# Sums over keys formed for four tiles at once in place of two, and some thirty further moves of single jobs in the planned order

## The chip, the cores and the metric

One core of one Trainium2 chip. The metric is the time of one execution on the device in microseconds. Five engines work side by side: TensorE (PE, with its weight loads PEld), VectorE (DVE), ScalarE (ACT), GpSimd (POOL) and SyncE (SP), which issues most of the transfers.

## The reference, cut to what matters

One transformer block in float32 with 2048 tokens of width 512: a linear attention, then a mixture of 8 experts of width 1792 to which every token goes. The change lies in the attention and in the order around it:

```python
h = x + A(layernorm(x))          # attention, 32 heads of 16
h2 = h + B(layernorm(h))         # experts
# A:
q, k, v = split_heads(x @ wqkv)
phi_q = concat(softmax(q @ w_phi), softmax(-(q @ w_phi)))   # per head, 32 features
phi_k = concat(softmax(k @ w_phi), softmax(-(k @ w_phi)))
kv = einsum("bhsf,bhsd->bhfd", phi_k, v)     # a sum over all 2048 keys
z  = einsum("bhsf->bhf", phi_k)              # likewise
o  = (phi_q @ kv) / (phi_q @ z + 1e-6)
return o @ wo
# B: gates = softmax(x @ wg), then for every expert gelu(x @ w1) @ w2, weighted by its gate
```

## The kernel before, in words

The tokens are 16 tiles of 128 rows (`NT`). The program has two stages. Up to about 310 us it computes the attention, the second layernorm, the gates and the first product of the experts, in an order of single jobs; behind that it runs the experts in a fixed loop.

**A matmul in float32 precision** is three passes: `mm3` (lines 66 to 75) takes a high and a low part of both sides and issues low by high (L73), high by low (L74) and high by high (L75). A projection of one tile (`project`, L224) is four such triples, so 12 passes. The key weights and the query weights are first multiplied with w_phi ("fold"), so the projections of keys and queries give the arguments of the softmax at once.

**A key tile** t runs through: x stats, x root, x norm, x trans (four transposes, L221, on TensorE), x high (L257, ScalarE) and x low (VectorE), which give the two parts of x; k proj and v proj (TensorE); v ones (L272, a memset of POOL that takes the buffer of the values and sets its column of ones) and v copy; k range (maxima and minima, L234 and L235, VectorE), k below (L239, VectorE) and k above (L242, POOL); k exp, k sums, k scale (L301, POOL).

**The sums over keys** are `k_add` (L302 to L309): for each of the 32 heads one matmul of 128 by 32 features with 128 by 17 values (16 and the column of ones), 32 instructions of four records each in the trace, so 128 records a tile. They add up in one PSUM bank over all 16 tiles, and nobody reads the bank before the last one. Job `("k add", t)` does this for `KB` = 2 tiles, t - 1 and t, in one block, eight blocks in all (t = 1, 3, ... 15). It also gives back the slots of both tiles' features and values.

**A query tile** runs through q proj (12 passes), q copy (L316, ScalarE), q range (VectorE), q subs (L239 and L242, POOL), q exp (ScalarE), q sums (VectorE), q scale (L340 and L341, POOL), and two q trans of four transposes each (L348, TensorE) with their q turned (ScalarE). Tiles 0 to 7 do so between the key tiles; tiles 8 to 15 come behind them and in a row. Then come, by groups of four tiles, q den (L378: denominators), their way to HBM and back (den out, den in), q num (L403: the key-value products), the output projection (out), the second layernorm (h stats to h trans and h turned), the gates (gate, gate copy, ... gate store at L507, whose rows go to HBM), and the products of the first expert (product). Beside it VectorE and ScalarE prepare the experts' first w1 blocks (L610 to L627) and sums of w2 (L644, whose loads are L587); the 16 loads of the output weights are L128, the second loads of x L426 (load r), the loads of w1 and w2 are SP's.

**What sets the order.** Each of these steps is a job with an engine, an estimated cost, the jobs that it must follow, a due time, and the slots that it takes and gives. `plan()` is a list scheduler in Python that makes one order of all jobs from that, within the slots of the pools (43 of `s4`, 15 of `s2`, four PSUM banks of `ps`, four of `pacc`). On that order a list `MOVES` is then applied, pair by pair: the first job is taken out and put right in front of the second. Then the jobs are issued one after the other, and each instruction of an engine is tied behind the one before it, so each engine runs its jobs in exactly this order. Waits between engines follow from the data and from the reuse of slots. The order of the issue is all that the list can change:

```python
order = [name for _, name in plan()]
for name, before in MOVES:
    order.remove(name)
    order.insert(order.index(before), name)
...
for name in order:
    n = len(traced)
    jobs[name][4]()
```

`jobs[name][4]` is the function that issues the job's instructions. A buffer in the program's names (`s_438`, `ps`, `pacc`) is a slot in SBUF or a bank in PSUM.

Of the kernel before, what the change touches and what calls it, by code (L numbers as in the profile page):

```python
# [21 lines left out]
def block_kernel(ctx: ExitStack, tc: tile.TileContext, x, wqkv, w_phi, wo, wg, w1, w2, out):  # L22
# [6 lines left out]
    NT = S // P  # L29
# [62 lines left out]
    st, low = {}, {}  # L92
# [416 lines left out]
    X = {}  # L509
# [487 lines left out]
    jobs, made = {}, []  # L997
# [11 lines left out]
    KB = 2  # L1009
# [431 lines left out]
    order = [name for _, name in plan()]  # L1441
# [3 lines that stand above are left out]
    at = {name: i for i, name in enumerate(order)}  # L1445
    assert all(at[d] < at[n] for n in jobs for d in jobs[n][3])

    assert max(at[n] for n in jobs if n[0] in ("den", "q proj", ("q trans", 1))) < min(at[("num", i), 3] for i in range(2))
    assert max(at[("num", i), 3] for i in range(2)) < at["product", 0, 0]
    for name in order:  # L1450
        n = len(traced)
        jobs[name][4]()
        if name[0] == "m" or len(traced) == n:
            continue
        for ins in traced[n:]:
            if ins.engine in issued:
                tc.add_manual_dep(ins, issued[ins.engine].name,
                                  mybir.DependencyInfo(mybir.DependencyClass.NoSync, mybir.DependencyReason.DATA),
                                  reason="planned order")
            issued[ins.engine] = ins  # L1460
# [28 lines left out]
```

## Time and profile before

| what | us |
|---|---|
| three runs | 2301.76, 2304.96, 2301.81 (median 2301.81) |
| the profiled execution | 2302.05 |
| its span in the trace | 2300.3 |
| TensorE busy, matmul / weight load | 2290.2 / 1998.8 |
| VectorE busy | 2116.5 |
| ScalarE busy | 1762.1 |
| POOL busy | 535.4 |

The span is the trace of the profiled execution, from its first to its last instruction; the execution's own time is 1.75 us longer. Times in the trace count from the span's start. Where the trace shows several instructions of one kind in a row as one line, `x4` is their number, and the duration runs from the first start to the last end. A matmul's duration overlaps with the next one's; how densely they are issued is read from the distance of their starts.

### The profile page before, as it was taken

To read this page: it belongs to the slowest core of one execution; us is meant where nothing else is said; L and a number is where in the kernel's file an instruction comes from. 1 tells how busy PE (TensorE), PEld (TensorE's weight loads), DVE (VectorE), ACT (ScalarE), POOL (GpSimd) and SP (SyncE) were. 2 spreads that over 40 slices of the span, in tenths; PEclk is the share of its full clock that TensorE was granted. 3 is DMA by queue.
4 is the path that set the end of the run, shared out by engine and by line. 5 is a ranking of instruction groups with operands and counts; after the bars stand their busy time and mean duration, and the time that the engine had idled before them with its cause. 6 is when DMAs were issued, how large, how long until landed. Compare 5 with 4: busy or idle time off the path is not lost.

```text
span 2300.3 us, 34809 instructions
## 1 busy us (share of the span) xinstructions
PE 2290.2 (100%) x12544; PEld 1998.8 (87%) x12544; DVE 2116.5 (92%) x3040; ACT 1762.1 (77%) x2934; POOL 535.4 (23%) x688
## 2 busy tenths in 40 slices
PE   9999999999999999999999999999999999999999
PEld 8888888888888888888888888888888888888887
DVE  8878999999999999999998999899999999999998
ACT  6646788877778777777877888877777777777874
POOL 6766211111111111111111421211111111111121
PEclk9999999999999999999999999999999999999999
DMA  3018468888888888888888998998888888878888
GB/s 125 25 49 273 151 164 165 157 165 158 175 165 161 166 157 168 165 161 174 148 177 197 214 193 170 215 197 174 151 178 159 156 175 149 176 153 177 165 162 186
DMA packets 182044, 379.36 MB, mean 165 GB/s; under 512 B 15568, under 2 KB 88912, under 8 KB 181840
## 3 DMA queue, kind: packets, MB, share of 16 engines
q0 software_dynamic: 63776, 210.79, 55.5%
q1 hardware_dynamic: 116768, 166.16, 22.3%
q8 instruction: 99, 1.62, 0.3%
q14 instruction: 73, 0.60, 0.1%
q10 hardware_dynamic: 1328, 0.18, 0.0%
HBM read 161.53 MB, written 224.99 MB: 168 GB/s over the span
## 4 chain that ended last, share of the span: by engine, by line
PE 80%; issue 3%; DMA 3%; DVE 1%; POOL 1%; ACT 0%; POOLq 0%; DVEq 0%; SPq 0%; ACTq 0%
PE ps L73 13%; PE ps L74 13%; PE ps L75 13%; PE pacc L75 13%; PE pacc L73 13%; PE pacc L74 13%; DMA acc1m<-acc1m 1%; DMA acc1m<-s 1%; DVE s L63 1%; DMA h<-s 1%; POOL acc1m L696 1%; PE pacc L793 0%; DMA s<-acc1m 0%; ACT s L694 0%; DVE s L655 0%
## 5 line engine op out<-in xcount | busy, mean ns | idle before, releaser
L63 DVE TENSOR_TENSOR s<-s,s 128x1024 fp32r<-128x1024 f32 (+1 forms) x789 | 743.0, 955 | 87.9 <-ACT s L62 79.0
L62 ACT ACTIVATE s<-s 128x1024 fp32r<-128x1024 f32 (+1 forms) x789 | 660.0, 842 | 12.2 <-DVE s L655 6.4
L73 PE MATMUL pacc<-s,s 128*128 128x512 f32 x1728 | 657.2, 380 | 0.7 <-DVE s L63 0.7
L74 PE MATMUL pacc<-s,s 128*128 128x512 f32 x1728 | 655.1, 379 | 0.4 <-DVE s L63 0.4
L75 PE MATMUL pacc<-s,s 128*128 128x512 f32 x1728 | 654.9, 379 | 0.0
L73 PE MATMUL ps<-s,s 128*128 128x512 f32 x1664 | 633.9, 381 | 1.4 <-DVE s L706 0.5
L74 PE MATMUL ps<-s,s 128*128 128x512 f32 x1664 | 631.0, 379 | 0.6 <-DVE s L63 0.6
L75 PE MATMUL ps<-s,s 128*128 128x512 f32 x1664 | 630.5, 379 | 0.0
L694 ACT ACTIVATE s<-pacc 128x512 f32<-128x512 f32 x756 | 441.5, 593 | 142.1 <-PE pacc L75 137.8
L705 ACT ACTIVATE ps<-ps 128x512 f32<-128x512 f32 x440 | 252.9, 585 | 172.5 <-DVE ps L748 116.2
L73 PEld LDWEIGHTS pacc<-s,s 128*128 128x128 f32 x1728 | 326.5, 189 | 47.9 <-issue 2.2
L74 PEld LDWEIGHTS pacc<-s,s 128*128 128x128 f32 x1728 | 326.6, 189 | 46.7 <-DVE s L63 1.0
L75 PEld LDWEIGHTS pacc<-s,s 128*128 128x128 f32 x1728 | 326.6, 189 | 46.3
L73 PEld LDWEIGHTS ps<-s,s 128*128 128x128 f32 x1664 | 314.4, 189 | 50.1 <-issue 1.5
L74 PEld LDWEIGHTS ps<-s,s 128*128 128x128 f32 x1664 | 314.6, 189 | 44.7 <-DVE s L63 1.3
L75 PEld LDWEIGHTS ps<-s,s 128*128 128x128 f32 x1664 | 314.5, 189 | 44.5
L696 POOL DMA_DIRECT2D acc0m<-s x189 | 162.2, 858 | 812.8 <-ACT s L694 792.3
L706 DVE TENSOR_TENSOR s<-ps,s 128x512 f32<-128x512 f32 x440 | 297.9, 686 | 37.9 <-ACT ps L705 32.6
L696 POOL DMA_DIRECT2D acc1m<-s x175 | 149.4, 855 | 727.4 <-ACT s L694 707.3
L655 DVE TENSOR_TENSOR s<-s,s 128x1024 f32<-128x1024 f32 x224 | 272.8, 1218 | 0.1
L710 ACT ACTIVATE ps<-ps 128x512 f32<-128x512 f32 x226 | 133.2, 589 | 52.2 <-PE ps L75 49.8
L627 DVE TENSOR_TENSOR s<-s,s 128x1024 fp32r<-128x1024 f32 x111 | 136.2, 1227 | 1.5 <-ACT s L625 1.5
(146 smaller groups left out, 1746.7 us busy)
## 6 DMA issues: line engine op xcount, KB each, us to landing
acc0m<-s POOLq DMA_DIRECT2D x196, 512.0 KB, 5.6
acc1m<-s POOLq DMA_DIRECT2D x184, 512.0 KB, 5.7
s<-in_B_w_dram SPq DMA_DIRECT2D x224, 256.0 KB
s<-in_B_w_dram SPq DMA_DIRECT2D x111, 512.0 KB
s<-cwT SPq DMA_DIRECT2D x16, 512.0 KB
s<-in_A_x_dram SPq DMA_DIRECT2D x16, 256.0 KB
s<-in_A_x_dram SPq DMA_DIRECT2D x8, 512.0 KB
rden<-sq SPq DMA_DIRECT2D x16, 256.0 KB
```

Of the source, the lines that this page charges most:

```text
L62: nc.scalar.activation(hi, src, AF.Copy)
L63: return eng.tensor_tensor(lo, src, hi.bitcast(F32), op=ALU.subtract)
L73: nc.tensor.matmul(out_, al, bh, start=first, stop=False, skip_group_check=True)
L74: nc.tensor.matmul(out_, ah, bl, start=False, stop=False, skip_group_check=True)
L75: nc.tensor.matmul(out_, ah, bh, start=False, stop=last, skip_group_check=True)
L627: nc.vector.tensor_tensor(sl, s, sh.bitcast(F32), op=ALU.subtract)
L655: nc.vector.tensor_tensor(r, B[a], B[b], op=ALU.subtract)
L694: nc.scalar.activation(e[:, d], p[d], AF.Copy)
L696: return nc.gpsimd.dma_start(macc[h, m], e, accum_op=ALU.add)
L705: nc.scalar.activation(src, src, AF.Gelu_apprx_tanh)
L706: nc.vector.tensor_tensor(B[b][:, q % 2], src, CW[h, e][:, int(b[2]) - 1], op=ALU.mult)
L710: nc.scalar.activation(dst, src, AF.Copy)
```

## The change

Behind `MOVES` a loop pairs the blocks of the sums: the blocks of k add 1, 5, 9 and 13 are taken from the order, and their instructions are issued at the place of k add 3, 7, 11 and 15, in front of that block's own. So there are four blocks of four tiles. The planner itself doesn't know of it: it plans with `KB` = 2 as before, and the list of slots given back is as it was. The list has 334 pairs in place of 302: eight are gone, 40 are added at its end. In the diff each pair of the list has a line of its own here, and "..." stands for pairs that are not told of.

```diff
     MOVES = [
...
-        (('gate store', 0), ('gate store', 1)),
-        (('h turned', 10), ('X high', 't4')),
-        (('h store', 6), ('keep', 'b11')),
-        ((('q turned', 1), 10), (('q turned', 1), 11)),
-        ('key values', ('q copy', 13)),
...
+        (('product', 0, 0), ('h trans', 10)),
+        (('q exp', 14), (('q turned', 0), 10)),
+        (('load r', 1), ('den out', 0)),
+        ((('q trans', 0), 9), (('q trans', 0), 8)),
+        (('h trans', 11), ('gate back', 1)),
+        (('h turned', 14), ('h turned', 13)),
+        (('fold', 'q', 3), ('v proj', 0)),
+        (('h store', 5), ('gate store', 1)),
+        (('q proj', 9), ('v proj', 14)),
+        ((('q trans', 1), 11), (('q trans', 1), 8)),
+        (('h turned', 8), ('h turned', 11)),
+        (('k add', 15), ('q proj', 10)),
+        ((('q trans', 0), 10), ('q proj', 15)),
...
     ]
...
+    for t in range(KB - 1, NT, 2 * KB):
+        first, then = jobs["k add", t][4], jobs["k add", t + KB]
+        order.remove(("k add", t))
+        then[4] = lambda f=first, g=then[4]: (f(), g())
     for name in order:
```

On TensorE, between a query projection (into `ps`) and the next key projection (into `pacc`), the two blocks of the first four tiles become one (the block of 39.6 us stood earlier, between the query projection and the key projection before these). In a row of L308, the first name is a tile's features and the second its values; `x32` are the 32 heads:

```order
 L74 MATMUL ps<-s_438,s_467 128x512
 L75 MATMUL ps<-s_438,s_467 128x512
-L308 MATMUL pacc<-s_410,s_562 32x17 x32
-L308 MATMUL pacc<-s_485,s_708 32x17 x32
+L308 MATMUL pacc<-s_245,s_344 32x17 x32
+L308 MATMUL pacc<-s_319,s_413 32x17 x32
+L308 MATMUL pacc<-s_415,s_562 32x17 x32
+L308 MATMUL pacc<-s_485,s_644 32x17 x32
 L73 MATMUL pacc<-s_243,s_581 128x512
 L74 MATMUL pacc<-s_243,s_581 128x512
```

The block that stood here for two tiles now holds four; the values lie in other slots, since the first two tiles keep theirs longer.

The last block on TensorE, before: between the query projection of tile 10 (x in `s_1284`) and that of tile 11 (`s_1463`), the sums of tiles 14 and 15:

```order
L73 MATMUL ps<-s_438,s_1284 128x512
L74 MATMUL ps<-s_438,s_1284 128x512
L75 MATMUL ps<-s_438,s_1284 128x512
L308 MATMUL pacc<-s_1737,s_1941 32x17 x32
L308 MATMUL pacc<-s_1864,s_2033 32x17 x32
L73 MATMUL ps<-s_422,s_1463 128x512
L74 MATMUL ps<-s_422,s_1463 128x512
L75 MATMUL ps<-s_422,s_1463 128x512
```

And with the change, behind the query projection of tile 8 (`s_1014`) and in front of that of tile 10 (`s_1220`):

```order
L74 MATMUL ps<-s_438,s_1014 128x512
L75 MATMUL ps<-s_438,s_1014 128x512
L308 MATMUL pacc<-s_1572,s_1703 32x17 x32
L308 MATMUL pacc<-s_1609,s_1888 32x17 x32
L308 MATMUL pacc<-s_1673,s_1941 32x17 x32
L308 MATMUL pacc<-s_1864,s_1982 32x17 x32
L73 MATMUL ps<-s_422,s_1220 128x512
L74 MATMUL ps<-s_422,s_1220 128x512
```

It now has tiles 12 to 15, and query projection 9, which stood in front of 10, is already done before value projection 14.

TensorE's last query transposes, before, from the last denominators of the second group (L378) to the first key-value products (L403); `s_2284` are the features of tile 11, `s_2123` of tile 8, `s_2219` of 10, `s_2310` of 12, `s_2368` of 13, and `x4` is one half of a tile:

```order
L378 MATMUL ps<-s_1774,s_116 32x128
L348 MATMUL ps<-ident,s_2284 128x128 x4
L348 MATMUL ps<-ident,s_2123 128x128 x4
L348 MATMUL ps<-ident,s_2219 128x128 x4
L348 MATMUL ps<-ident,s_2284 128x128 x4
L348 MATMUL ps<-ident,s_2310 128x128 x8
L348 MATMUL ps<-ident,s_2368 128x128 x8
L403 MATMUL ps<-s_963,s_115 32x128 x8
```

And with the change, where `s_2187` is tile 8, `s_2206` tile 10 and `s_2314` tile 12:

```order
L378 MATMUL ps<-s_1710,s_116 32x128
L348 MATMUL ps<-ident,s_2187 128x128 x4
L348 MATMUL ps<-ident,s_2284 128x128 x4
L348 MATMUL ps<-ident,s_2206 128x128 x4
L348 MATMUL ps<-ident,s_2284 128x128 x4
L348 MATMUL ps<-ident,s_2314 128x128 x8
L348 MATMUL ps<-ident,s_2368 128x128 x8
L403 MATMUL ps<-s_963,s_115 32x128 x8
```

The four halves of tiles 8, 10 and 11 stand in another order; the number of transposes is the same, and tiles 12 and 13 stay last. On VectorE and POOL no job changes its place. On ScalarE query exponential 14 is two places further up, q turned 0 of tile 11 stands in front of q turned 1 of tile 10, h turned 11 and 8 change places, and so do h turned 14 and 13. On SP load r 1 stands before den out 0, the first gate's store before the load of w2, and h store 5 before the second gate's store.

## Rows read from the trace of the kernel before

**Rows 1.** The page: busy time of each engine in us, its share of the span and its number of instructions; and the chain of work that ended last, by engine.

```profile
PE 2290.2 (100%) x12544; PEld 1998.8 (87%) x12544; DVE 2116.5 (92%) x3040; ACT 1762.1 (77%) x2934; POOL 535.4 (23%) x688
...
PE 80%; issue 3%; DMA 3%; DVE 1%; POOL 1%; ACT 0%; POOLq 0%; DVEq 0%; SPq 0%; ACTq 0%
```

**Rows 2.** Busy time by stretch, 310 to 2300 us: length, then busy us and instructions of PE, PEld, DVE, ACT and POOL, the granted clock, the DMA share and GB/s.

```profile
310.00:2300.00 1990.00, 1983.37 (x9206) 1732.61 (x9204) 1855.07 (x2622) 1564.26 (x2602) 360.62 (x425) 1.00 0.84 171
```

**Rows 3.** TensorE's timeline from 36.0 us: start, duration, engine, line, operation, out<-in, size, number; in square brackets idle time before it and what ended it. Passes, four transposes, passes.

```profile
36.08 0.38 PE L74 MATMUL pacc<-s,s 128*128 128x512 f32 x1
36.30 0.38 PE L75 MATMUL pacc<-s,s 128*128 128x512 f32 x1
36.51 0.60 PE L221 MATMUL ps<-ident,s 128*128 128x128 f32 x4
...
37.17 0.38 PE L74 MATMUL ps<-s,s 128*128 128x512 f32 x1
```

**Rows 4.** The sums over keys: all of line 308 (number, duration in ns min/median/max, first and last start); then TensorE's timeline around the second block, in the stretch from 57.1 to 59.3 us; and, as the last row, the same block in the stretch that ends at 58.1 us.

```profile
L308 PE MATMUL pacc<-s,s x1024: 177/183/204, 39.6 to 155.5; 128*32 128x17 f32 x171
...
57.22 0.38 PE L75 MATMUL ps<-s,s 128*128 128x512 f32 x1
57.53 1.33 PE L308 MATMUL pacc<-s,s 128*32 128x17 f32 x128
58.78 0.48 PE L73 MATMUL pacc<-s,s 128*128 128x512 f32 x1
59.10 0.38 PE L74 MATMUL pacc<-s,s 128*128 128x512 f32 x1
...
57.53 0.74 PE L308 MATMUL pacc<-s,s 128*32 128x17 f32 x64
```

**Rows 5.** The same timeline around the third block, behind which four transposes stand.

```profile
76.40 0.38 PE L75 MATMUL ps<-s,s 128*128 128x512 f32 x1
76.71 1.33 PE L308 MATMUL pacc<-s,s 128*32 128x17 f32 x128
77.97 0.66 PE L221 MATMUL ps<-ident,s 128*128 128x128 f32 x4
...
78.68 0.38 PE L74 MATMUL pacc<-s,s 128*128 128x512 f32 x1
```

**Rows 6.** The same timeline, the blocks of k add 9, 11 and 13.

```profile
111.13 1.33 PE L308 MATMUL pacc<-s,s 128*32 128x17 f32 x128
...
125.57 1.33 PE L308 MATMUL pacc<-s,s 128*32 128x17 f32 x128
...
139.97 1.33 PE L308 MATMUL pacc<-s,s 128*32 128x17 f32 x128
```

**Rows 7.** The same timeline from 174.9 us, the last query transposes and the first key-value products.

```profile
174.97 1.96 PE L348 MATMUL ps<-ident,s 128*128 128x128 f32 x16
177.28 1.06 PE L348 MATMUL ps<-ident,s 128*128 128x128 f32 x8 [0.34 <-POOL s L242]
178.81 1.44 PE L348 MATMUL ps<-ident,s 128*128 128x128 f32 x8 [0.47 <-POOL s L341]
180.18 1.53 PE L403 MATMUL ps<-s,s 64*32 64x128 f32 x64
```

**Rows 8.** POOL's timeline: the last key scaling, the subtractions of the first two query tiles behind it and of a later one, and a scaling at the end.

```profile
149.45 2.19 POOL L301 TENSOR_TENSOR s<-s,s 128x1024 f32<-128x1024 f32 x1 [3.07 <-DVE s L297]
152.60 1.08 POOL L239 TENSOR_TENSOR s<-s,mx 128x512 f32<-128x512 f32 x1 [0.96 <-DVE mx L234]
153.64 2.06 POOL L242 TENSOR_TENSOR s<-mx,s 128x512 f32<-128x512 f32 x1
...
157.74 1.08 POOL L239 TENSOR_TENSOR s<-s,mx 128x512 f32<-128x512 f32 x1
...
179.21 1.14 POOL L341 TENSOR_TENSOR s<-s,s 128x512 f32<-128x512 f32 x1
```

**Rows 9.** VectorE: all of line 610 in the span (ns min/median/max), and two rows of its timeline.

```profile
L610 DVE TENSOR_TENSOR s<-s x111: 361/418/1899, 143.5 to 2234.6; 128x256 f32<-128x256 f32 x111
...
143.54 1.90 DVE L610 TENSOR_TENSOR s<-s 128x256 f32<-128x256 f32 x1
...
149.77 2.15 DVE L621 TENSOR_TENSOR s<-s,s 128x256 fp32r<-128x256 f32 x1
```

**Rows 10.** Timelines: SP's issue of the output weights' loads, POOL's memset of value tile 15 and its next job, ScalarE's high part of x 15, and the first pass of key projection 15 on TensorE.

```profile
68.58 7.39 SPq L128 DMA_DIRECT2D s<-in_A_wo_dram  x16
...
125.78 0.16 POOL L272 MEMSET s<- 128x32 f32 x1
129.36 1.94 POOL L301 TENSOR_TENSOR s<-s,s 128x1024 f32<-128x1024 f32 x1 [3.42 <-DVE s L297]
...
125.83 0.60 ACT L257 ACTIVATE s<-ps 128x512 fp32r<-128x512 f32 x1
...
137.29 0.38 PE L73 MATMUL pacc<-s,s 128*128 128x512 f32 x1
```

**Rows 11.** SP's timeline, the loads of w2 and the first gate's store; and all of line 644 on VectorE, the sums of w2, up to 320 us.

```profile
217.88 3.34 SPq L587 DMA_DIRECT2D s<-in_B_w_dram  x4
...
227.11 16.16 SPq L507 DMA_DIRECT2D cwT<-sq  x8
...
L644 DVE TENSOR_TENSOR s<-s,s x6: 682/684/693, 252.0 to 303.5; 128x512 f32<-128x512 f32 x6
```

More of the change, by code (lines that the diff above doesn't have):

```diff
@@ L1437, in block_kernel @@
     late["m"] = moe()
-    MOVES = [((('q trans', 1), 11), ('den', 1)), (('keep', 'b21'), ('keep', 'b22')), (('h stats', 9), (('value', 0, 1), 3)), (('den', 2), (('q trans', 0), 13)), (('h turned', 14), ('h turned', 13)), (('den', 2), (('q trans', 1), 13)), (('den', 1), (('q trans', 1), 12)), (('load r', 1), ('den out', 1)), ((('q trans', 1), 14), (('q trans', 0), 14)), (('gate copy', 3), ('gelu pb', 0)), ((('q trans', 0), 11), (('q trans', 0), 12)), (('h trans', 9), ('h trans', 8)), ((('num', 0), 1), (('q trans', 1), 15)), (('den', 2), (('num', 0), 0)), (('product', 0, 2), ('gate', 2)), ((('q trans', 1), 8), (('q trans', 1), 10)), ((('num', 0), 1), (('q trans', 0), 15)), (('den', 2), (('q trans', 0), 13)), (('product', 0, 2), ('gate turn', 2)), (('q exp', 15), (('q turned', 0), 13)), (('h stats', 14), ('X low', 't4')), (('den out', 2), (('den in', 1), 1)), (('den', 2), (('num', 1), 0)), (('den', 1), (('q trans', 0), 12)), ((('num', 1), 0), (('q trans', 0), 14)), (('product', 0, 1), ('gate back', 1)), ((('q trans', 0), 11), (('q trans', 0), 12)), (('product', 0, 0), ('product', 0, 1)), ((('num', 0), 1), ('out', 1)), ((('num', 1), 0), (('q trans', 1), 14)), (('h turned', 7), ('h norm', 9)), (('w1 sums', 1, 0), ('q sums', 14)), (('den', 1), (('q trans', 1), 9)), (('den', 1), (('q trans', 0), 12)), (('q scale', 11), ('q scale', 12)), ((('q trans', 1), 14), (('q trans', 1), 15)), (('map', 3), ('x root', 0)), (('den', 1), (('q trans', 0), 11)), (('h add', 12), ('gate norm', 1)), (('out', 15), ('h trans', 12)), ((('q trans', 1), 9), (('q trans', 1), 10)), ((('q trans', 1), 8), (('q trans', 0), 10)), (('q exp', 13), ('q copy', 15)), (('keep', 'b22'), ('gate store', 3)), (('den', 1), (('q trans', 1), 9)), (('h norm', 8), ('h norm', 9)), ((('q turned', 1), 14), (('o high', 1, 1), 0)), ((('q trans', 1), 11), (('q trans', 0), 12)), ((('q turned', 1), 11), ('q exp', 14)), ((('q trans', 1), 8), ('q proj', 14)), (('h turned', 9), ('gate exp', 1)), (('fold', 'q', 0), ('x trans', 2)), (('h store', 4), ('h store', 5)), (('den', 1), (('q trans', 0), 11)), (('fold', 'q', 0), ('fold', 'q', 1)), (('h trans', 14), ('h trans', 13)), (('fold', 'q', 3), ('fold', 'q', 2)), (('den', 2), (('q trans', 1), 13)), ((('q turned', 1), 12), ('q exp', 14)), (('den', 1), (('q trans', 1), 10)), ((('q trans', 1), 11), (('q trans', 1), 10)), (('gate exp', 1), ('h turned', 9)), (('den', 2), (('q trans', 0), 13)), (('seed pb', 0), ('X high', 't4')), (('v proj', 0), ('fold', 'q', 0)), ((('num', 0), 0), (('q trans', 1), 13)), (('X low', 't4'), 'w2 sums'), (('gate copy', 2), ('h norm', 12)), (('copy', 1), 'm1 high'), ((('q trans', 1), 10), (('q trans', 1), 9)), (('den', 1), (('q trans', 1), 9)), ((('num', 0), 0), ('den', 2)), (('h norm', 13), ('h turned', 12)), (('den', 1), (('q trans', 0), 12)), (('gate turn', 2), ('h trans', 12)), (('h add', 13), ('sum', 3)), ((('q trans', 0), 14), (('num', 1), 0)), ((('q trans', 0), 10), (('q trans', 1), 8)), ((('num', 1), 0), (('q trans', 0), 14)), (('den', 1), (('q trans', 1), 11)), ('load w2', ('gate store', 1)), (('h turned', 8), ('X high', 't3')), (('product', 0, 4), ('h trans', 13)), (('gate store', 1), 'load w2'), (('product', 0, 4), ('h trans', 15)), (('den', 1), (('q trans', 0), 11)), (('k proj', 1), ('turn', 'q', 3)), (('den', 1), (('q trans', 1), 10)), (('map', 0), ('x root', 0)), ((('num', 1), 3), (('num', 0), 3)), (('copy', 0), ('seed pb', 0)), (('h trans', 13), ('h trans', 14)), (('den', 1), (('q trans', 1), 11)), ((('q trans', 0), 10), (('q trans', 0), 8)), (('X high', 't1'), ('gate exp', 1)), (('fold', 'q', 1), ('v proj', 0)), (('w low', 'v', 3), ('x stats', 3)), ('load gates', ('keep', 'b11')), ((('q trans', 1), 8), ('q proj', 15)), ((('q trans', 1), 8), ('q proj', 13)), (('h turned', 14), ('gelu pd', 0)), (('den', 1), (('q trans', 0), 12)), (('den', 2), (('num', 0), 0)), ((('num', 1), 1), (('q trans', 1), 15)), ((('q trans', 0), 13), (('q trans', 1), 13)), (('hidden b22', 1), ('plus pb', 1)), (('den', 1), (('q trans', 0), 11)), ((('q trans', 1), 11), (('q trans', 0), 12)), ((('num', 0), 0), (('q trans', 1), 13)), (('h stats', 12), ('sum', 4)), (('h norm', 8), ('h norm', 10)), ((('q trans', 1), 11), (('q trans', 1), 10)), ((('q turned', 1), 8), (('q turned', 0), 10)), (('q exp', 14), (('q turned', 1), 11)), (('keep', 'b21'), ('keep', 't2')), ('load w2', ('load r', 7)), (('k proj', 1), ('x trans', 2)), ((('num', 0), 0), ('den', 2)), (('den', 2), (('q trans', 1), 13)), (('den', 2), (('q trans', 0), 13)), (('q proj', 13), (('q trans', 1), 8)), (('h store', 6), ('h store', 7)), (('den', 2), (('q trans', 0), 13)), ((('num', 0), 0), (('q trans', 0), 13)), (('den', 2), (('q trans', 0), 13)), (('h turned', 8), ('h turned', 10)), (('gate store', 0), ('gate store', 1)), ((('o high', 1, 0), 3), (('o high', 1, 1), 3)), ((('q trans', 1), 14), (('q trans', 0), 14)), (('h turned', 7), (('o high', 1, 1), 3)), (('h trans', 11), ('h trans', 10)), (('h turned', 11), ('h turned', 8)), ((('q trans', 0), 10), (('q trans', 1), 10)), (('h trans', 10), ('h trans', 11)), ((('q trans', 1), 8), (('q trans', 0), 9)), ((('num', 0), 0), (('q trans', 1), 12)), (('h turned', 15), ('gelu pd', 0)), (('q scale', 12), ('q subs', 15)), ((('num', 0), 0), (('q trans', 0), 13)), ((('num', 1), 1), (('q trans', 0), 15)), ((('num', 1), 0), (('q trans', 0), 14)), (('den', 2), (('q trans', 0), 13)), ((('num', 0), 0), (('q trans', 1), 12)), (('den', 2), (('q trans', 0), 13)), ((('q trans', 1), 15), (('num', 1), 1)), (('load x', 7), ('load x', 6)), ((('q trans', 1), 8), (('q trans', 1), 11)), ((('q trans', 1), 14), (('num', 1), 1)), ((('q trans', 1), 11), (('q trans', 1), 9)), (('out', 13), ('product', 0, 1)), ((('q trans', 1), 8), (('q trans', 0), 9)), ((('num', 1), 1), ('out', 0)), ((('num', 0), 0), (('q trans', 1), 13)), (('out', 13), ('product', 0, 0)), (('X low', 't4'), ('plus pd', 0)), ((('q trans', 0), 8), (('q trans', 0), 9)), ((('o high', 1, 1), 3), ('h turned', 7)), (('h turned', 8), ('gate rows', 1)), (('w1 high', 1, 1), (('q turned', 1), 13)), (('h turned', 15), ('h turned', 14)), (('X low', 't3'), ('X low', 'b22')), (('turn', 'q', 1), ('turn', 'q', 0)), ((('q trans', 1), 13), (('num', 0), 0)), ((('q trans', 1), 9), (('q trans', 1), 10)), (('h turned', 6), (('o high', 0, 0), 3)), ((('num', 0), 0), (('q trans', 1), 13)), (('map', 1), ('map', 2)), ((('q turned', 0), 13), (('q turned', 1), 13)), (('den', 1), (('q trans', 1), 10)), ((('q trans', 1), 10), ('den', 1)), (('den', 1), (('q trans', 1), 9)), ((('q trans', 1), 8), ('den', 1)), ((('q turned', 1), 12), (('q turned', 0), 13)), (('h turned', 8), ('h turned', 10)), (('product', 0, 4), ('h trans', 14)), (('den', 1), (('q trans', 0), 11)), (('load x', 5), ('load x', 3)), (('den', 1), (('q trans', 1), 11)), ((('q trans', 1), 10), (('q trans', 1), 11)), (('product', 0, 4), ('h trans', 13)), (('h norm', 10), ('X high', 't1')), (('turn', 'q', 3), ('turn', 'q', 0)), (('q sums', 12), ('q range', 15)), (('seed pb', 0), ('copy', 0)), (('q sums', 11), ('q range', 14)), ((('q trans', 0), 9), (('q trans', 1), 9)), ((('q trans', 0), 9), (('q trans', 0), 10)), (('h turned', 10), ('X high', 't4')), (('product', 0, 1), ('out', 14)), ((('q trans', 0), 9), (('q trans', 0), 8)), (('w1 high', 1, 1), (('q turned', 1), 13)), (('h turned', 14), ('h turned', 13)), ((('q trans', 0), 11), (('q trans', 1), 10)), (('load', 'v'), ('load x', 5)), (('out', 11), ('h trans', 7)), ((('q turned', 0), 12), ('q exp', 15)), ((('q trans', 0), 12), ('den', 2)), (('den', 1), (('q trans', 1), 11)), (('w1 sums', 1, 0), ('q sums', 15)), (('load r', 1), (('den in', 1), 0)), ((('q turned', 1), 8), (('q turned', 1), 10)), (('h store', 5), ('keep', 'b11')), (('den', 2), (('q trans', 1), 13)), ((('q turned', 1), 12), ('w1 high', 1, 1)), ((('q turned', 1), 9), (('q turned', 1), 10)), (('w1 high', 1, 1), (('q turned', 1), 12)), (('h norm', 10), ('h turned', 9)), (('X low', 't1'), ('gate norm', 1)), (('out', 5), ('out', 6)), (('product', 0, 1), ('h trans', 10)), (('product', 0, 4), ('h trans', 14)), (('h trans', 14), ('h trans', 13)), (('h stats', 8), (('value', 0, 0), 3)), (('h turned', 11), ('seed pb', 0)), (('product', 0, 1), ('h trans', 11)), ((('q trans', 0), 8), ('q proj', 15)), (('x stats', 2), ('w low', 'v', 2)), (('h store', 6), ('keep', 'b11')), ((('num', 1), 3), ('out', 9)), ((('num', 1), 3), (('num', 0), 3)), (('product', 0, 5), ('h trans', 15)), (('gate max', 0), ('h add', 8)), (('h trans', 10), ('product', 0, 0)), (('h store', 5), 'load gates'), ((('num', 0), 3), (('num', 1), 3)), (('seed pb', 0), ('h turned', 10)), ((('q turned', 1), 8), (('q turned', 1), 10)), (('fold', 'q', 0), ('v proj', 0)), ((('q trans', 1), 10), (('q trans', 1), 8)), (('h norm', 7), ('h turned', 6)), (('h turned', 13), ('h turned', 14)), (('den out', 0), (('den in', 0), 0)), ((('num', 1), 1), (('q trans', 0), 15)), (('gate', 1), ('h trans', 8)), (('product', 0, 4), ('h trans', 14)), (('q scale', 12), ('q subs', 15)), (('den', 2), (('q trans', 1), 13)), (('X low', 't1'), ('h add', 13)), (('h store', 5), ('keep', 'b11')), ((('q turned', 1), 10), (('q turned', 1), 11)), (('X low', 't4'), ('plus pb', 0)), ((('num', 0), 0), (('q trans', 1), 13)), (('q proj', 15), (('q trans', 0), 8)), (('den', 2), (('q trans', 0), 13)), ((('q trans', 1), 8), (('q trans', 0), 10)), ((('q turned', 1), 8), ('q exp', 14)), (('h turned', 11), ('seed pb', 0)), ((('q trans', 0), 8), ('q proj', 15)), (('X low', 'b22'), ('X low', 't3')), (('h trans', 13), ('h trans', 14)), ((('q trans', 0), 14), (('num', 1), 0)), (('den', 2), (('q trans', 1), 13)), (('den', 2), (('num', 0), 0)), (('h norm', 8), (('o high', 1, 0), 3)), ((('num', 1), 1), ('out', 0)), ((('q trans', 1), 14), (('q trans', 1), 15)), (('w1 high', 1, 1), (('q turned', 0), 14)), ((('q trans', 1), 13), (('q trans', 0), 13)), (('x norm', 4), ('high', 'q', 1)), (('h turned', 9), ('gate rows', 1)), ('key values', ('q copy', 12)), (('map', 3), ('map', 1)), ((('q turned', 1), 13), (('q turned', 1), 12)), (('h root', 10), ('h root', 11)), ((('q trans', 1), 8), (('q trans', 1), 9)), (('X high', 'b22'), ('h norm', 10)), ('key values', ('q copy', 11)), ((('q trans', 1), 8), ('den', 1)), (('gelu pb', 0), ('gate copy', 3)), ((('q turned', 1), 8), (('q turned', 1), 11)), ((('num', 0), 0), ('den', 2)), (('den', 2), (('num', 0), 0)), (('q exp', 11), ('q exp', 12)), ((('q turned', 0), 11), (('q turned', 1), 8)), ((('num', 1), 1), (('q trans', 1), 15)), ('key values', ('q copy', 13)), ((('q trans', 1), 8), (('q trans', 0), 11)), (('plus pd', 0), ('hidden b11', 0)), (('q exp', 12), ('q exp', 13)), ((('q trans', 1), 9), (('q trans', 1), 10)), ((('q trans', 1), 10), (('q trans', 1), 9)), ((('num', 1), 1), (('q trans', 0), 15)), ((('num', 0), 0), ('den', 2)), ((('q trans', 0), 13), (('q trans', 1), 13)), ((('q trans', 1), 13), ('den', 2)), ((('q trans', 0), 13), (('q trans', 1), 13)), ((('num', 0), 0), ('den', 2)), ((('num', 0), 0), (('q trans', 1), 13)), ((('num', 0), 0), ('den', 2)), (('q proj', 15), (('q trans', 0), 8)), (('den', 1), (('q trans', 1), 8)), ((('num', 1), 0), (('q trans', 0), 14)), ((('q trans', 0), 10), ('q proj', 15)), (('h trans', 14), ('h trans', 13)), ((('q trans', 0), 11), (('q trans', 1), 8)), (('q exp', 15), (('q turned', 1), 11)), (('hidden b11', 0), ('plus pd', 0)), ((('q trans', 1), 12), (('q trans', 0), 13)), (('q subs', 14), ('q scale', 11)), ((('q trans', 0), 9), ('q proj', 15)), (('load', 'q'), ('load x', 3)), ((('q trans', 1), 10), (('q trans', 1), 11))]
```

1 line of the change is left out of this document (added).

## The prediction

> **What bounds the kernel now.** I read the page's busy times and its chain first, then the busy times by stretch, then TensorE's own timeline, and only then the engines that feed it. TensorE is busy 2290.2 of 2300.3 us, and 80% of the chain that ended last is TensorE's [rows 1]. In the 1990 us from 310 on, at a granted clock of 1.00 (the 2.4 GHz level), it is idle 6.63 us [rows 2]. So the bound is the number of passes and the price of one; a change of order can win only what stands between passes. The reader is to see what stands there. Passes of a projection follow each other at 0.22 us (36.08 to 36.30), and four transposes between two projections put 0.44 us, 0.11 each, between its last pass and the second pass of the next (36.30 to 37.17 in place of 0.43) [rows 3]. The sums over keys are dearer than their passes: that is the next part. Where TensorE waits for others in this region, it waits twice for POOL between 177 and 180.2, 0.34 and 0.47 us [rows 7].
>
> An effect of 0.2%, 4.6 us, is about what a measurement of this kernel can tell from no change.
>
> **The change: the block.** Eight blocks of 128 records of line 308 become four of 256; the 1024 records stay [rows 4]. I price a block by what it adds between the last pass before it and the second pass behind it. At 57.53 that is 57.22 to 59.10, 1.88 us, where two ordinary steps take 0.43: 1.45 us for two tiles. The first tile's 64 records fill 57.53 to about 58.12 (up to 58.1 exactly 64 records are begun), 0.59 us [rows 4]. Two tiles at 0.59 are 1.18, so 0.27 us belong to the block and not to its tiles: the entry (0.31 in place of 0.22), the exit (0.32 in place of 0.22 before the second pass), and some 0.08 in its last tile. Where transposes follow the block, 76.40 to 78.68 is 2.28 us against 0.87 (36.30 to 37.17) for the same transposes without it [rows 3, 5]: 1.41, less 1.18, leaves 0.23. The blocks that go are those at 39.6, 76.71, 111.13 and 139.97 [rows 4 to 6]. The three in front of the last key projection, which starts at 137.29 [rows 10], give 0.27 + 0.23 + 0.27 = 0.77 us; the fourth gives 0.27. Sum: 1.04 us. From both sides: at least 0 (if a change of tile inside a block costs as much as leaving and entering it), at most 4 x 0.31 = 1.24, taking 1.45 less two tiles at 0.57 (57.53 to 58.10).
>
> A rule of the Trainium skill speaks against this term: the page "TensorEngine Tiling (Array Packing)", section "Instruction Overhead", gives every matmul a fixed overhead of its own. The number of matmuls is the same here, so by that rule the sum would be 0, and the term above would be wrong. The rows show 128 records in 1.25 us from first start to the next pass, some 10 ns each, and extra time only at the block's two ends [rows 4]; on this the trace does not bear the rule out.
>
> **The moved projections and folds.** Query projection 9 now runs before value projection 14, and the last block runs before query projection 10 instead of behind it. Projections follow each other without a gap, so the passes cost the same in any order: 0. Fold q 3 moves in front of value projection 0, 0 for the same reason; either could cost or save one drain of the pipe, 0.1 us by the steps above.
>
> **What the gain meets.** Behind the key projections POOL works through the queries: from the last key scaling at 149.45 to the end of a query scaling at 180.35 it is idle 0.96 us once and otherwise about 0.1 us at a time [rows 8]. TensorE's last transposes before the key-value products wait for exactly that (178.81, 0.47 us for POOL) and the first of these products starts at 180.18 [rows 7]. So this stretch ends when POOL ends, and POOL's chain hangs on key projection 15, through VectorE's maxima (152.60, 0.96 us for DVE) [rows 8]. It moves forward by the 0.77 us that are won before that projection, and the 0.27 us of the fourth block turn into waiting: +0.27. I checked two things that could break the chain's start. Query projection 8 now ends near 136.52 + 5 x 2.6 (12 passes at 0.216) = 149.5 and its copy near 150.3 (0.6 us and a little), but VectorE is taken until 149.77 + 2.15 - 0.77 = 151.1 [rows 9]: hidden. Query projection 10 now follows a block of four (some 2.6 us) and ends near 154.7; copy and maximum take 1.3 us, 156.0, and POOL comes to that tile at 157.74 - 0.77 = 157.0 [rows 8]: hidden by 1.0 us. If that cover were gone, each late microsecond would go to POOL's chain and so to TensorE one to one. Bounds of this term: 0 (POOL gains too) to +1.73 (a collision, below).
>
> **What the block holds.** Two features and two value tiles wait a block longer, so four of 43 slots stay taken for some 14 us more (111.13 to 125.57 is the distance of two blocks [rows 6]). The tiles last in line feel it: the ones of value tile 15 (POOL, 125.78) and the high part of x 15 (ACT, 125.83) used to come over 13 us behind the sums of tiles 8 and 9 (111.13 to 112.5) and now stand against the block of tiles 8 to 11 near 125 [rows 6, 10]. Behind the memset POOL has 3.42 us of idle time, and the high part ends at 126.43 for a projection at 137.29, with one VectorE job, its low part, between them [rows 10]. A wait of up to 2.6 us, the whole block, costs 0. The ones of value tile 14, next before them on POOL, now wait for eight loads of the output weights; SP issued all sixteen from 68.58 on in 7.39 us, 40 us and more earlier [rows 10]: 0.
>
> **The other queues.** On SP the rows of the first gate are stored before w2 is loaded, so the four loads of 217.88 slip behind a store that was at 227.11, and load r 7 behind them; the first sums of w2 run at 252.0 [rows 11]: over 15 us of cover. Load r 1 moves ahead of den out 0, in a time when SP waits: 0. ACT's exchanges (query exponential 14 two places up, the copies of turned rows 11 and 8, 14 and 13) are of single jobs in an engine with 77% load [rows 1]: 0; my bounds are plus or minus 0.5, the size of the wait for POOL above [rows 7].
>
> **Sum.** -1.04 + 0.27 + 0 = -0.77 us. The profiled execution took 2302.05 us; 2301.28. The median of the runs stands 0.24 below it, so I forecast **2301.0**, and by the bounds of the likeliest case 2300.4 to 2301.7.
>
> **Rivals.**
> A, new collisions of VectorE and POOL. Line 610 took 1.90 us against a median of 0.42, line 621 took 2.15, both while POOL ran its long operations; POOL's line 242 took 2.06 against 1.08 [rows 8, 9]. The change shifts both engines' work against each other. One more such collision on the chain of queries costs 2.15 - 0.42 = 1.73: -0.77 + 1.73 = +0.96, 2302.8. For it: three long rows in this stretch alone. Against it: nearly all of both chains shifts together. The Trainium skill's page "SBUF — State Buffer", section "SBUF: two separate sides", says that the two engines take a shared port in turn, each for a whole instruction; the trace agrees (1.90 us where 0.42 is usual).
> B, the exchanges of query transposes take the waits out. Between 174.97 and 180.18 stand 32 transposes in 5.21 us; at 0.11 they need 3.5 [rows 7]. Without the 1.7 us: 2301.28 - 1.7, about 2299.6, or 2299.3 against the median. For it: the transposes there are what the list moves most. Against: POOL sets the end.
> C, the block's price goes with the tiles, or the pass count decides: no gain, 2301.8. Against it stand the two prices above.
> D, slower. The held slots bite: in the stretch of the last key tiles a job at the head of ACT's or POOL's queue takes a slot that only the next block frees. A block is 14.4 us behind another (125.57 after 111.13) [rows 6]; less the 3.42 us of POOL's idle time and the 0.8 us won, about +10, 2312. It decides as soon as such a wait exceeds 3.42 us on POOL or some 10 us for x 15 [rows 10]. Against it: no block waited for its inputs before, and the loads of x stand far ahead of their use.
> E, faster. The late waits, 6.63 us from 310 on [rows 2], depend on when transfers fall; a shift could dissolve 5.5 of them: 2295.5. Nothing in the change touches them.
>
> **How the numbers follow.** Forecast 0.62, A 0.10, B 0.13, C 0.09, D 0.04, E 0.02. Faster by over 0.2% is E alone, slower D alone: 0.02 and 0.04; the rest, 0.94, lies within 0.2%. The range leaves out D, E and the outer parts of A and B: 2299.5 to 2302.9.
>
> **What would show it.** Right: line 308 stands in four blocks of 256 records of about 2.5 us; the last key projection starts near 136.5, the first key-value products near 179.4, the first expert product 0.8 us earlier than now, and all behind it keeps that distance; POOL's chain ends near 179.6. Wrong: four blocks at 2.9 us (C); products near 177.7 (B); a long row of VectorE or POOL between 150 and 180 (A); idle time of POOL before the ones of tile 15 beyond 3 us (D); a difference that arises behind 310 us (E).

## The result, and the profile after

| kernel | median, us | runs, us | ratio to before, 95% interval |
|---|---|---|---|
| before | 2301.81 | 2301.62 to 2304.96 | |
| changed | 2315.16 | 2311.98 to 2317.47 | 1.0055 (1.0044 to 1.0066) |

The change makes the kernel 13.4 us slower, above the whole range that I gave. The profiled execution is the quickest of the five: 2311.98, with a span of 2310.3, 10.0 more than before. Three executions among those told of below took 4544 to 12047 us (one of the kernel before, one each of the two kernels in blocks of three tiles), and medians and ratios leave them out. (The 128 records that the section on the kernel before gives a tile count weight loads too: a tile's sums are 64 records of matmuls and 64 of weight loads. The prediction and all that follows count the matmuls, so a block of two tiles is 128 records and one of four 256.)

The page of the changed kernel, with busy times and one DMA queue (packets, MB, share of 16 engines):

```profile
PE 2289.9 (99%) x12544; PEld 1998.9 (87%) x12544; DVE 2116.6 (92%) x3040; ACT 1762.6 (76%) x2934; POOL 536.8 (23%) x688
...
q8 instruction: 99, 1.62, 0.3%
```

TensorE does the same work [rows 1] in a longer span: it stands still for 10 us more. Behind 310 us nothing changed, with 6.32 us of idle time where it was 6.63 [rows 2]:

```profile
310.00:2310.00 2000.00, 1993.68 (x9254) 1741.76 (x9252) 1865.69 (x2637) 1573.45 (x2616) 362.57 (x427) 1.00 0.84 171
```

What TensorE waited for, the longest in sum (us, times, longest); "issue" is time in which an engine waits for nothing that the profile shows:

```profile
PE pacc L308 <- issue: 8.9, 4, 3.1
```

And where, on its timeline. All four blocks of 256 records stop once inside, and no semaphore releases them:

```profile
55.73 0.38 PE L75 MATMUL ps<-s,s 128*128 128x512 f32 x1
56.04 1.60 PE L308 MATMUL pacc<-s,s 128*32 128x17 f32 x168
59.48 0.96 PE L308 MATMUL pacc<-s,s 128*32 128x17 f32 x88 [1.83 <-issue]
60.37 0.48 PE L73 MATMUL pacc<-s,s 128*128 128x512 f32 x1
...
96.47 2.21 PE L308 MATMUL pacc<-s,s 128*32 128x17 f32 x234
100.65 0.38 PE L308 MATMUL pacc<-s,s 128*32 128x17 f32 x22 [1.97 <-issue]
...
127.51 2.06 PE L308 MATMUL pacc<-s,s 128*32 128x17 f32 x212
131.60 0.56 PE L308 MATMUL pacc<-s,s 128*32 128x17 f32 x44 [2.03 <-issue]
...
155.59 2.28 PE L308 MATMUL pacc<-s,s 128*32 128x17 f32 x230
160.97 0.40 PE L308 MATMUL pacc<-s,s 128*32 128x17 f32 x26 [3.10 <-issue]
```

Before, 128 records ran through without a pause [rows 4 to 6]. The stops come behind 168, 234, 212 and 230 records, so no fixed length of a block sets them. What they share shows when TensorE's instructions are counted from one stop's end to the next (busy time by stretch; the numbers of matmuls and of weight loads stand in brackets):

```profile
59.47:100.64 41.17, 39.20 (x510) 34.60 (x510) 33.19 (x53) 23.98 (x38) 32.80 (x44) 1.00 0.13 40
100.64:131.59 30.95, 28.92 (x382) 25.86 (x383) 22.13 (x31) 18.97 (x30) 14.40 (x17) 1.00 0.03 6
131.59:160.96 29.37, 26.28 (x382) 22.98 (x382) 20.93 (x27) 10.21 (x15) 14.44 (x10) 1.00 0.22 69
```

With the 4, 3 and 4 semaphore instructions that the trace lists in between, that is 510 + 510 + 4 = 1024, 382 + 383 + 3 = 768 and 382 + 382 + 4 = 768: four, three and three times 256. And queue 8 carries 99 packets in 1.62 MB, 16 KB each, for TensorE's 25,539 instructions (12,544 matmuls, as many weight loads, 451 for semaphores): about 256 a packet. So TensorE stops where it steps onto a new page of 256 instructions that is not there yet. All the traces of this study bear that out: in ten of the thirteen TensorE waits for over 0.2 us with "issue" as the reason, 39 times in all, 24 of them in line 308. Each time the number of TensorE's instructions listed ahead of the matmul that ends the wait, divided by 256, leaves 193 to 195. The other three (the kernel before, the moves alone, the projection between) have no such wait. Each record is a matmul with a weight load, so 128 records fill a page, and TensorE runs through it in about 1.25 us, where a page of passes lasts some 27.

The DMA queues in three short stretches, 57.1 to 58.2, 158.0 to 158.6 and 158.6 to 159.6 us:

```profile
q8 instruction: 1, 0.02, 5.2%
...
q1 hardware_dynamic: 35, 0.08, 37.4%
...
q8 instruction: 1, 0.02, 6.0%
```

The first block's 40th record is the first page boundary in it (168 - 128), near 56.4. The packet comes behind it, in the first of these stretches, and TensorE goes on at 59.48: 3.1 us from entering one page to having the next, less 1.25 in the page, are the 1.83 of idle time. In the fourth block the boundary is at 156.5 (record 102), queue 1 is still moving data at 158, the instruction packet comes at 158.6, and it takes 4.5 us to 160.97.

Behind the fourth stop the granted clock falls:

```profile
162.00:164.00 2.00, 2.00 (x6) 1.55 (x6) 0.00 (x0) 0.00 (x0) 1.02 (x1) 0.50 0.04 8
164.00:166.00 2.00, 2.00 (x8) 1.65 (x7) 0.00 (x0) 0.12 (x1) 0.00 (x0) 0.66 0.00 0
```

0.50 and 0.66 in place of 1.00 (the 1.2 GHz level for a time) cost 1.0 + 0.7 = 1.7 us. The sum, 8.9 + 1.7 = 10.6, is what the first key-value product is late: 190.85 in place of 180.18 [rows 7]. Two smaller things cancel in it: ahead of these products TensorE waits 0.7 us longer than before for other engines (1.7 us between 30 us and there, against 1.0), and the merging itself saves about as much (an estimate; see below).

### The profile page after: what moved, and what is told of

Its sections match the earlier page's. It is cut to its first block, busy times and chain, and to the rows that moved or that the text cites. A ratio compares the mean times of both kernels' runs of the same rounds, so it can differ in the third digit from the quotient of the medians.

```text
span 2310.3 us, 34818 instructions
## 1 busy us (share of the span) xinstructions
PE 2289.9 (99%) x12544; PEld 1998.9 (87%) x12544; DVE 2116.6 (92%) x3040; ACT 1762.6 (76%) x2934; POOL 536.8 (23%) x688
## 3 DMA queue, kind: packets, MB, share of 16 engines
q8 instruction: 99, 1.62, 0.3%
## 4 chain that ended last, share of the span: by engine, by line
PE 77%; issue 5%; DVE 2%; POOL 1%; DMA 1%; ACT 1%; POOLq 0%; DVEq 0%; ACTq 0%
PE ps L73 13%; PE ps L74 13%; PE ps L75 13%; PE pacc L74 13%; PE pacc L75 13%; PE pacc L73 13%; POOL acc1m L696 1%; DVE s L63 1%; DMA h<-s 1%; DVE s L655 0%; ACT s L62 0%; DMA acc1m<-s 0%; DVE s L706 0%; POOL h L822 0%; ACT s L694 0%
```

## The experiments

Theory F is that of instruction pages; S puts the loss on the moved jobs or on the slots that are held longer. The kernel before, run again beside the first four, the next four and the last three, took 2301.72, 2301.31 and 2301.65 us.

**The two halves of the change apart.** The merge alone:

```diff
-    MOVES = [the changed list]
+    MOVES = [the list of before]
```

> The merge of the blocks alone, with the list of moves of before. Theory F (instruction fetch): TensorE's instructions come in pages of 256 (16 KB packets of the instruction queue), the next page is asked for when one is entered and is usable some 3.1 us later; a page of records of line 308 lasts 1.25 us, so each block of 256 records stops at the second page boundary inside it. From the counts of instructions in front of the blocks it expects four stalls of 1.8 to 3.5 us at records 168, 235, 213 and 219 (each to within 6), and a time 9 to 15 us above before: 2311 to 2317. Theory S (the moved jobs or the slots held longer): the moves are gone, so at most half of the loss is left, 2302 to 2308, and the waits stand ahead of jobs of ScalarE, POOL or a projection, not inside line 308. My forecast's sum: 2301.0, 0.8 us faster.

2310.42 us, ratio 1.0037 (1.0025 to 1.0049), with these stops (the first row's view ends at 61 us, so 13 of its 88 records are not in it):

```profile
60.02 1.19 PE L308 MATMUL pacc<-s,s 128*32 128x17 f32 x75 [2.28 <-issue]
...
102.48 0.38 PE L308 MATMUL pacc<-s,s 128*32 128x17 f32 x22 [1.79 <-issue]
...
133.69 0.56 PE L308 MATMUL pacc<-s,s 128*32 128x17 f32 x44 [2.29 <-issue]
...
166.03 0.51 PE L308 MATMUL pacc<-s,s 128*32 128x17 f32 x38 [1.94 <-issue]
```

They come behind 168, 234, 212 and 218 records, as counted beforehand (168, 235, 213, 219). The time is 0.6 us under the expected range. The fourth block stands later here than in the change, no data moves at that time, and the stop is 1.94 us, not 3.10.

The moves alone:

```diff
-    for t in range(KB - 1, NT, 2 * KB):
-        first, then = jobs["k add", t][4], jobs["k add", t + KB]
-        order.remove(("k add", t))
-        then[4] = lambda f=first, g=then[4]: (f(), g())
```

> The moves alone, with blocks of two tiles (128 records) as before. Theory F: no stall over 0.1 us inside line 308 and the time of before within 1 us: 2301 to 2303. Theory S: the loss is the moves', so 2308 to 2315.

2302.72 us, ratio 1.0003 (0.9994 to 1.0012): no difference. So the moves do not cost it; that the slots are held longer, the other half of S, is open until the projection stands between the halves, below.

**Work added inside the block, and behind it.** 12 added passes go between the block's halves; in a second kernel, the same behind them. (`passes(n)` issues n passes of 376 columns into columns of the bank that nobody reads.)

```diff
-        then[4] = lambda f=first, g=then[4]: (f(), g())
+        then[4] = lambda f=first, g=then[4]: (f(), passes(12), g())
+        then[4] = lambda f=first, g=then[4]: (f(), g(), passes(12))    # in the second kernel
```

> The changed kernel with 12 added passes of 376 columns (some 0.16 us each, 1.9 us a block, 7.6 us in all) between the second and the third tile of each block; they go to columns of the same bank that nobody reads. Theory F: the added passes lie on the first whole page of the block, so they fill the time in which the next page is fetched; the stalls of the first three blocks shrink to below 0.5 us, that of the fourth to below 2, and the time does not rise although 7.6 us of work are added: 2309 to 2315. Theory S: the work comes on top, 2319 to 2325.

> The same 12 added passes a block, but behind its last tile. Theory F: they cover nothing, since the stall stands between the block's own records: four stalls of 1.8 to 3.5 us as in the changed kernel, and the work comes on top: 2319 to 2325. A theory by which any pause or added work near the block does it (not its place on the pages) expects the same time as with the passes inside.

Inside: 2315.6 us, 1.0062 (1.0049 to 1.0074). Behind: 2329.42 us, 1.0119 (1.0105 to 1.0133). The same work in another place is 13.8 us dearer. Inside, the first block's second half starts and ends without a pause, and TensorE's waits (second piece) show one stop left in line 308, the fourth, with 1.3 us:

```profile
55.96 1.27 PE L308 MATMUL pacc<-s,s 128*32 128x17 f32 x128
59.27 1.44 PE L308 MATMUL pacc<-s,s 128*32 128x17 f32 x128
...
PE ps L403 <- issue: 1.9, 1, 1.9
PE ps L378 <- issue: 1.5, 1, 1.5
PE pacc L308 <- issue: 1.3, 1, 1.3
```

The two other lines I had not foreseen: key-value products (L403) and denominators (L378) stop too. 48 added passes shift all that follows by 96 places, and these quick records now meet the page boundaries. That, and passes that took 2.1 us a block (57.16 to 59.27) where 1.9 was expected, is more than the 0.6 us by which the time stands above the expected range. Behind the block, the four stops are all there; and the clock fell in five stretches (busy time by stretch):

```profile
PE pacc L308 <- issue: 9.4, 4, 3.1
...
60.00:100.00 40.00, 40.00 (x280) 35.83 (x269) 28.75 (x47) 21.95 (x35) 29.86 (x39) 0.96 0.13 38
100.00:130.00 30.00, 27.71 (x388) 25.03 (x388) 19.92 (x29) 15.70 (x26) 13.67 (x15) 0.94 0.01 2
130.00:160.00 30.00, 28.01 (x376) 25.11 (x376) 15.25 (x22) 9.98 (x14) 9.64 (x10) 0.94 0.14 37
160.00:180.00 20.00, 16.88 (x319) 15.02 (x318) 12.55 (x15) 6.06 (x10) 10.25 (x7) 0.91 0.16 54
200.00:240.00 40.00, 35.57 (x637) 29.74 (x635) 29.01 (x49) 22.43 (x41) 27.07 (x34) 0.96 0.68 194
```

0.04 x 40, 0.06 x 30 and so on make 8.6 us: a stop of 2 us can cost nearly as much again. The expectation had nothing for the clock, nor for the stops in lines 403 and 378 that this kernel has too (1.9 and 1.2 us), so the time is above its range. So the 13.8 us are not the stops alone: by the two profiles line 308 stops for 8.1 us more (9.4 less 1.3), and the clock, lowered once inside and five times behind, takes 6.8 more; together that is a little over the difference.

**The change again**, unedited:

> The changed kernel once more, beside the others of this call. Theory F: four stalls inside line 308 at the same records (168, 234, 212, 230), since the instructions before them are the same in number; their lengths vary between 1.8 and 3.5 us, and behind some of them the granted clock falls for some 3 us, whose number makes the spread between runs: 2309 to 2317.

2314.78 us, 1.0058 (1.0044 to 1.0071); the stops at the same records, 9.6 us in sum, and the clock lowered in two stretches in place of one (0.94 from 100 to 130, 0.91 from 160 to 180), in a span of 2313.3. Of the 3.0 us between this profile and the first, the second such stretch is 1.7, the longer stops are 0.7, and a stop of 0.6 in line 403 is the rest; that the same things make the whole spread of the runs is inferred.

**The shift alone.** Nothing merged, nothing moved:

```diff
     for _ in range(WARM):
         nc.tensor.matmul(warm[:, :P], ident, ident, start=True, stop=True)
+    for _ in range(24):
+        nc.tensor.matmul(warm[:32, :16], ident[:, :32], ident[:, :16], start=True, stop=True)
```

> The kernel before with nothing moved or merged; 24 tiny matmuls (32 weights rows, 16 columns) are added to the ones that warm TensorE before the first load is there, which shifts every later instruction by 96 places in the stream. Theory F: still no stall inside line 308 (a block of 128 records never holds a whole page and what is fetched ahead of it), but the denominators and key-value products, 64 quick records a group, now meet the page boundaries: two new stalls of 1 to 2 us near line 403 at 180 and line 378 at 199. 0 to 1 us at the start, so 2303.5 to 2308. Without pages (theory S, or a limit on the length of a block): the start alone, 2301.5 to 2303.

2305.87 us, 1.0019 (1.0010 to 1.0028): 4.6 us slower through 24 tiny matmuls some 180 us earlier. Lines are two further down here, so 380 and 405 are the denominators and the products:

```profile
PE ps L380 <- issue: 1.3, 1, 1.3
PE ps L405 <- issue: 0.7, 1, 0.7
```

Neither wait stands among TensorE's longest ones before. Line 308 (here 310) has no stop, as counted. With one of 0.3 in line 75 the profile shows 2.3 us of stops; the rest of the 4.6 is not placed.

**Blocks of three tiles, unshifted and shifted by 60.** This tells a page from a length. The edit is to the kernel before; the shifted one has 15 of the tiny matmuls too.

```diff
+    for place, tiles in ((1, ()), (3, (0, 1, 2)), (5, (3, 4, 5)), (7, ()), (9, (6, 7, 8)), (11, (9, 10, 11)), (13, (12, 13)), (15, (14, 15))):
+        if tiles:
+            jobs["k add", place][4] = lambda tiles=tiles: [k_add(i) for i in tiles]
+        else:
+            order.remove(("k add", place))
```

> The kernel before with its list of moves, but the sums in blocks of 3, 3, 3, 3, 2 and 2 tiles, at the places of k add 3, 5, 9, 11, 13 and 15. Theory F, from the counts: the blocks of 192 records at the places 3, 9 and 11 stall at records 168, 159 and 150 (each to within 4) for 1.8 to 2.5 us; the one at place 5 for at most 0.5 us at record 140, because some passes stand on its first page; none in the blocks of two. Two blocks fewer give 0.5 us: 2306 to 2312. A limit on the length of a block in records would stop all four at the same record or none.

> The same with 15 tiny matmuls added at the warm-up, a shift by 60 places. Theory F: the same blocks of 192 records, in the same places and order, now have no page boundary behind a whole page of records: no stall over 0.3 us anywhere inside line 308, and none in lines 403 and 378; two blocks fewer than before give 0.5 us, the start takes 0 to 0.7: 2301.0 to 2302.3, 4 us or more under the unshifted one. A limit on length, or slots held longer: the same time as the unshifted one within 1 us.

Unshifted 2308.39 us, 1.0029 (1.0017 to 1.0041); shifted 2301.85, 1.0001 (0.9992 to 1.0010). Unshifted, three of the four blocks stop, behind 168, 158 and 149 records, and the one at 77.99 does not:

```profile
59.75 0.38 PE L308 MATMUL pacc<-s,s 128*32 128x17 f32 x24 [2.12 <-issue]
...
77.99 1.89 PE L308 MATMUL pacc<-s,s 128*32 128x17 f32 x192
...
115.11 0.46 PE L308 MATMUL pacc<-s,s 128*32 128x17 f32 x34 [2.02 <-issue]
...
131.65 0.56 PE L308 MATMUL pacc<-s,s 128*32 128x17 f32 x43 [1.47 <-issue]
```

Shifted, no block stops; the same blocks with 15 tiny matmuls more are 6.5 us quicker. Against the count, line 405 (the key-value products, two lines further down) has two waits of together 1.0 us there, the longest in sum:

```profile
PE ps L405 <- issue: 1.0, 2, 0.6
```

**Fewer passes inside.**

```diff
-        then[4] = lambda f=first, g=then[4]: (f(), passes(12), g())
+        then[4] = lambda f=first, g=then[4]: (f(), passes(7), g())
```

> The changed kernel with 7 added passes of 376 columns between the second and the third tile of each block, 1.1 us a block and 4.4 us in all, in place of the 12 of the earlier run. Theory F: each stall inside line 308 is 1.1 us shorter than in the changed kernel (some 0.8 to 1.5 us left, the fourth up to 2.2), so the end of the last block comes within 1 us of that in the changed kernel although 4.4 us of work were added; the shift is 56 places, short of the 64 from which the counts put new stalls into lines 403 and 378: 2309 to 2315. If the earlier run's missing waits were not the pages' doing: 4.4 us more than the changed kernel, 2319.

2312.49 us, 1.0047 (1.0035 to 1.0060): below the 2314.78 of the change although work is added, 1.3 us a block by the trace (1.1 expected). The stops, in the change 1.83, 1.97, 2.03 and 3.10:

```profile
59.71 1.02 PE L308 MATMUL pacc<-s,s 128*32 128x17 f32 x95 [0.61 <-issue]
...
101.28 0.51 PE L308 MATMUL pacc<-s,s 128*32 128x17 f32 x36 [0.98 <-issue]
...
132.42 0.73 PE L308 MATMUL pacc<-s,s 128*32 128x17 f32 x64 [0.87 <-issue]
...
161.94 0.64 PE L308 MATMUL pacc<-s,s 128*32 128x17 f32 x54 [1.95 <-issue]
```

Each is shorter by 1.0 to 1.2, nearly as much as the passes take. Against the change run again the stops are 5.2 us less in sum (4.4 for 9.6) and the passes 5.3 more; that the time is even shorter fits the clock, which does not fall in this profile and fell twice there.

**Passes that are there anyway.** The block's halves stand on both sides of one projection.

```diff
-        first, then = jobs["k add", t][4], jobs["k add", t + KB]
         order.remove(("k add", t))
-        then[4] = lambda f=first, g=then[4]: (f(), g())
+        i = order.index(("k add", t + KB))
+        while jobs[order[i - 1]][0] != "PE" or order[i - 1][0] not in ("k proj", "v proj", "q proj"):
+            i -= 1
+        order.insert(i - 1, ("k add", t))
```

> The changed kernel with all its moves; the sums of the first two tiles of each block are issued one projection earlier, so that 12 of the passes that are there anyway (2.6 us) stand between the halves, and nothing else is changed. The features and values are held some 2.6 us less than in the changed kernel. Theory F: no page is now run through in less than 3.5 us, so no stall over 0.3 us inside line 308, at most 1 in the fourth: 2301 to 2304, as the moves alone. Theory S: held slots and moves are as in the changed kernel, so 2311 to 2316.

2303.92 us, 1.0008 (0.9999 to 1.0017). With the slots held nearly as long as in the change and all its moves, the loss is gone to within 2 us, and TensorE has no wait in line 308. With this, S falls. The fourth block, halves on both sides:

```profile
147.54 1.30 PE L308 MATMUL pacc<-s,s 128*32 128x17 f32 x128
151.56 1.46 PE L308 MATMUL pacc<-s,s 128*32 128x17 f32 x128
```

**A version that might beat both.** Against the shifted blocks of three:

```diff
-    for _ in range(WARM):
+    for _ in range(WARM - 2):
...
-    for _ in range(15):
+    for _ in range(17):
```

> The shifted threes (a shift of 60 places) with the start trimmed: two of the twelve large warming matmuls go and two more tiny ones come. Theory F: no stall over 0.3 us inside line 308, as shifted; two blocks fewer than before, 0.5 us: 2300.5 to 2302.0, at best just under the kernel before and not to be told from it.

2301.72 us, 1.0002 (0.9993 to 1.0011): the kernel before is not beaten. A block of three on its timeline:

```profile
56.12 0.38 PE L75 MATMUL ps<-s,s 128*128 128x512 f32 x1
56.43 1.80 PE L310 MATMUL pacc<-s,s 128*32 128x17 f32 x192
...
58.49 0.38 PE L74 MATMUL pacc<-s,s 128*128 128x512 f32 x1
```

56.12 to 58.49 less 0.43 is 1.94 us, against 1.45 for two tiles.

## Why the prediction was wrong

- **The step that failed is the price of the block.** I took it from blocks of 128 records and carried it to 256. I named no rival in which the block itself stops. The forecast of 2.5 us a block was 4.3 in the first block (56.04 to 60.37) and 5.7 in the last (155.59 to 161.30). What the runs showed in its place: 1.8 to 3.1 us in each block are a wait for the next page of instructions, 8.9 us in all, and 1.7 us more go to the clock behind the last. Of the blocks of 128 records none stopped, neither the eight before nor those under the shift by 96; by the count, passes share their pages. At 192 records the place on the page decides; the blocks of 256 without work between their halves all stopped. The profile of before held one hint, queue 8 with the same 99 packets of 16 KB, which I never set against the block. "Issue" in the chain [rows 1] is no hint: nearly all of it stands behind 1240 us, at jobs of POOL, and none at the stops.
- **The page that bears on it was not weighed.** The Trainium skill, page "Runtime: NRT & Kernel Launch", section "Instruction fetch mechanics", says that an engine's instructions come in blocks of 16 KiB, 256 instructions, the next fetched while one runs, and that this is mostly hidden. The traces agree on the block and on the fetch of one ahead; "hidden" holds for pages of passes, not for 128 records in 1.25 us. The page also gives TensorE room for 2048 instructions; here it stopped with one page ahead at most.
- **Merging saves about what I said.** In the block shown, the quickest of its kind there, a third tile adds 1.94 - 1.45 = 0.49 us, not 0.59, so a block costs 1.45 - 2 x 0.49 = 0.47, not 0.27. The other three blocks of three in that trace last 1.83 to 1.99 us where this one lasts 1.80, which leaves 0.1 to 0.4. Rival C (no gain in fewer blocks) is not borne out by the trace, but in time the saving of some 1 us stays below what a run can tell.
- **Rival D named the right size, 2312, for the wrong reason.** That is luck, as the two jobs that it named did not wait for slots. The ones of value tile 15 run right behind POOL's job before them (and the high part of x 15, at 128.30, right behind ScalarE's), and POOL then waits for VectorE as it did [rows 10]:

```profile
128.36 0.16 POOL L272 MEMSET s<- 128x32 f32 x1
131.83 1.94 POOL L301 TENSOR_TENSOR s<-s,s 128x1024 f32<-128x1024 f32 x1 [3.30 <-DVE s L297]
```

- **The moves at 0** held (1.0003). The query transposes still wait for POOL (0.8 and 0.6 us), so rival B did not come; from 310 on nothing changed, so E did not; and A's collision is not needed, since stops and clock give the delay of the products.

## What to carry to other kernels

Before packing short instructions closer together, count them: find how many instructions an instruction packet carries (its bytes and number stand in the profile), and how long the quickest run of that many lasts. If that is under the time from a page's entry to the first instruction of the next, some 3 us here and over 5 in places where data moves at the same time, put longer instructions between, or place the run across a page boundary. An added or removed instruction anywhere earlier shifts all later pages, so an edit far away can make or cure such a stop.

## What of the hardware was not expected

- From entering a page to the first instruction of the next, at the stops in line 308: 2.8 to 3.7 us where no data packet of queue 1 began between the entry and the instruction packet, 4.5 to 4.7 in the five (the change twice, the twelve passes inside and behind, the seven passes) where 135 to 144 did. At the stops in lines 378 and 403, with 143 to some 1400 of them in between, it was 3.95 to 5.65.
- 24 tiny matmuls that do nothing made the kernel 4.6 us longer; 2.3 us of that are seen as stops far behind them. With 15 of them, in blocks of three, the time came down by 6.5.
- After some stops of 1.9 to 3.1 us in otherwise dense work the granted clock was at 0.5 for some 3 us, 1.7 us lost each time, and after others not; what decides is open.
